# Moving where TensorE's stationary tiles lie in SBUF relative to x

## The chip, the cores and the metric

The kernel runs on one core of one Trainium2 chip. The metric is the device time of one execution in microseconds (us); lower is better. Before the change it is 855.13 us, the median of three runs that lie between 854.54 and 855.58 us.

## What is computed

The inputs q, k and v have 8 batches, 8 heads, 576 positions and 64 features each, in fp32. An attention without a score matrix is followed by a two-layer network:

```python
q_s = softmax(q, axis=features)            # per position
k_s = softmax(k, axis=positions)           # per feature
kv  = einsum('bhsd,bhse->bhde', k_s, v)    # 64x64 per batch and head
x   = einsum('bhsd,bhde->bhse', q_s, kv)   # then laid out as 4608 tokens x 512
h   = x @ w_in                             # 512 -> 2048
g   = h * sigmoid(1.702 * h)
out = g @ w_out                            # 2048 -> 512
```

## The kernel before, in words

**Precision.** Every operand of the two large products is held as a pair, a high part rounded to the type fp32r and a low part that holds what the rounding left, and each product is three fp32r matmuls: high by high, high by low, low by high. On TensorE, a matmul has a stationary operand (128x128, read from SBUF by its own instruction, LDWEIGHTS) and a moving operand (128 rows by 256 or 512 columns, read from SBUF while it streams).

**Tiling.** The 4608 tokens are cut into nine blocks t of 512. The 2048 hidden features are cut into eight pairs p of two groups of 128. In a block, eight steps handle the eight pairs: p goes up from 0 to 7 in even blocks and down from 7 to 0 in odd ones (`pair`, line 384).

**First layer.** In blocks 0 and 1 `plain1` (line 786, matmuls on line 794) takes x whole: 512 moving columns, stationary operand `wj`. In blocks 2 to 8 `ffn1` (line 825, matmuls on line 841) uses seven products of 256 moving columns in place of eight, on sums and differences of the halves of x and of w_in. Product 6, 7, 5 and 4 take their stationary operand from the tile `wt` (sums of w_in), product 1, 2 and 3 from `wj` (w_in itself). Each product is six matmuls, so that a step has 24 with `wt` and 18 with `wj`. The moving operands are the tiles `xo`, which lie in the same places as the tiles `xp` of the first blocks.

**Double buffers.** There are two tiles `wt0` and `wt1`, and two pairs of tiles `wj00`, `wj01` and `wj10`, `wj11`; step p uses those with the number p % 2. They are loaded again from DRAM for each step (`load_kept`, line 389), except where the next step has the same pair.

**Second layer.** `ffn2` (line 889, matmuls on line 904) has the activations `gh` and `gl` as stationary and w_out (`w`, 512 columns) as moving operand: 24 matmuls for each step, interleaved with the first layer's of the next step.

**Attention.** For each block, line 634 forms kv, line 683 transposes q (moving operand: the identity matrix `ident`, stationary operand: `qt`) and line 704 forms x (moving `qT`, stationary `kvn`).

**Order.** The order of the work on each engine comes from `Plan`, a list scheduler with the costs and due times of lines 19 to 125, which runs when the kernel is built. It knows tiles by name and not by address.

**Addresses.** All SBUF tiles come from one pool and are never freed; `sb` (line 193) allocates a tile on its first call, and tiles follow one another in the order of these calls. Nearly all tiles take a multiple of 512 bytes in each partition. The exceptions are the four `vt` and the one `vl` with 2080 bytes, `r`, `qm0` and `qm1` with 32 bytes, and `first` with 64. The first tile, `ident`, begins 128 bytes above a multiple of 512. So the address of every tile modulo 512 is 128 plus the odd bytes of the exceptions that were allocated ahead of it. Addresses inside the tiles of the large products step by multiples of 512, so a tile's residue holds for each matmul that reads it. Before the change, the residues are:

| tile | role | residue modulo 512 | x lies above it by |
|---|---|---|---|
| `xo`, `xp`, `w` | moving, both layers | 448 | - |
| `gh`, `gl` | stationary, second layer | 128 | 320 |
| `wt0` (memory shared with `wide`) | stationary, first layer | 384 | 64 |
| `wj00`, `wj01`, `wj10`, `wj11` | stationary, first layer | 384 | 64 |
| `wt1` (allocated when first used) | stationary, first layer | 448 | 0 |
| `qt`, `qT` | stationary of line 683, moving of line 704 | 256 | - |
| `ident`, `kvn`, `kt` | moving of line 683, stationary of lines 704 and 634 | 128 | - |

Of the kernel before, what the change touches and what calls it, by code (L numbers as in the profile page):

```python
# [10 lines left out]
F32R = mybir.dt.float32r  # L11
# [125 lines left out]
def efficient_attention_then_gelu_ffn(  # L137
# [28 lines left out]
    B, H, S, D = q.shape  # L166
    NTOK, DM = out.shape
    FF = w_out.shape[0]
    P = 128
    C = 4  # L170
# [3 lines left out]
    NP = H // 2  # L174
    KC = DM // P
# [3 lines left out]
    CM = SM // P  # L179
    ST = S - SM  # L180
    W = D + 1
# [11 lines left out]
    def sb(name, shape, dtype=F32, tag=None):  # L193
        return const.tile(shape, dtype, name=name, tag=tag or name)
# [5 lines left out]
    tt = sb("tt", [P, 4, HT])  # L200
    tmp = [sb(f"tmp{i}", [P, DM]) for i in range(2)]
    kt = [sb(f"kt{i}", [P, 2, CM, D]) for i in range(NP)]
    vt = [sb(f"vt{i}", [P, 2, CM, W]) for i in range(NP)]
    qt = [sb(f"qt{i}", [P, C, 2, D]) for i in range(NP)]
    qT = [sb(f"qT{i}", [P, TB]) for i in range(2)]
    mx = [sb(f"mx{i}", [P, 2, D]) for i in range(NP)]
    m1 = sb("m1", [P, 2, 2, D])
    qm = [sb(f"qm{i}", [P, 2 * C]) for i in range(2)]
    r_ = sb("r", [P, 2, NP])
    rs = [r_[:, i] for i in range(2)]  # L210
    kl, vl = sb("kl", [P, H, D]), sb("vl", [P, H, W])
    wj = [[sb(f"wj{i}{jj}", [P, 2, KC, P], F32R) for jj in range(2)] for i in range(2)]
    wts = {}

    def wt(i):
        if i not in wts:
            wts[i] = sb(f"wt{i}", [P, 2, 4, 2 * P], F32R, tag=f"wt{i}")
        return wts[i]


    wide = sb("wide", [P, 4, DM], tag="wt0")
    kept = [[dram.tile([P, 2 * DM], F32, name=f"kept{p}{jj}") for jj in range(2)] for p in range(NS)]
    kept_t = [dram.tile([P, 4 * DM], F32, name=f"kept_t{p}") for p in range(NS)]

# [779 lines left out]
```

## Time and profile before

| what | value |
|---|---|
| median of three runs | 855.13 us |
| the profiled execution's own time | 853.69 us |
| its span (first to last instruction) | 851.9 us |
| TensorE's granted clock | 1.00 of full speed |
| TensorE matmuls busy | 843.5 us |
| VectorE busy | 525.6 us |
| ScalarE busy | 487.2 us |
| GpSimd busy | 114.3 us |

The profile gives for each engine the time in which it was busy, for each group of like instructions their number, their total and their mean duration, and for any stretch of the span the busy time of each engine in it. Matmuls are pipelined: a matmul's own duration is longer than the distance from its start to the next one's start, so the rate of TensorE is read from starts, not from durations. A timeline row gives the start of the first of several like instructions that follow one another, and their number.

### The profile page before, as it was taken

To read this page: it belongs to the slowest core of one execution; us is meant where nothing else is said; L and a number is where in the kernel's file an instruction comes from. 1 tells how busy PE (TensorE), PEld (TensorE's weight loads), DVE (VectorE), ACT (ScalarE), POOL (GpSimd) and SP (SyncE) were. 2 spreads that over 40 slices of the span, in tenths; PEclk is the share of its full clock that TensorE was granted. 3 is DMA by queue.
4 is the path that set the end of the run, shared out by engine and by line. 5 is a ranking of instruction groups with operands and counts; after the bars stand their busy time and mean duration, and the time that the engine had idled before them with its cause. 6 is when DMAs were issued, how large, how long until landed. Compare 5 with 4: busy or idle time off the path is not lost.

```text
span 851.9 us, 14617 instructions
## 1 busy us (share of the span) xinstructions
PE 843.5 (99%) x5643; PEld 722.3 (85%) x5644; DVE 525.6 (62%) x1082; ACT 487.2 (57%) x833; POOL 114.3 (13%) x175
## 2 busy tenths in 40 slices
PE   9999999999999999999999999999999999999998
PEld 4687787778888898888888998899888899889986
DVE  8899896999627875467554765375356533453333
ACT  5799769768537758465744675464356433343322
POOL 1000020120113011111211121100110011101110
PEclk9999999999999999999999999999999999999999
DMA  9999935893479467564845665623654165416541
GB/s 290 283 339 359 265 132 187 263 320 133 129 233 239 129 161 223 173 186 100 246 158 163 165 184 171 177 88 116 204 162 138 50 198 174 148 50 198 173 148 50
DMA packets 127845, 155.63 MB, mean 183 GB/s; under 512 B 76576, under 2 KB 105760, under 8 KB 121376
## 3 DMA queue, kind: packets, MB, share of 16 engines
q0 software_dynamic: 25248, 83.37, 31.7%
q1 hardware_dynamic: 102528, 71.32, 28.2%
q8 instruction: 45, 0.74, 0.4%
q14 instruction: 24, 0.20, 0.1%
HBM read 128.45 MB, written 26.21 MB: 182 GB/s over the span
## 4 chain that ended last, share of the span: by engine, by line
PE 87%; DVE 6%; DMA 4%; ACT 1%; issue 1%; POOL 0%; SPq 0%; DVEq 0%; ACTq 0%; POOLq 0%
PE bank L904 42%; PE bank L841 33%; PE bank L794 5%; DMA raw<-in_moe_w_out 3%; PE bank L634 2%; PE bank L704 2%; PE bank L683 2%; PE bank L296 1%; DVE w L368 1%; DVE gl L812 1%; DVE wide L333 1%; DVE raw L337 0%; PE bank L582 0%; PE bank L583 0%; DMA vt<-in_v 0%
## 5 line engine op out<-in xcount | busy, mean ns | idle before, releaser
L904 PE MATMUL bank<-w,gh 128*128 128x512 f32 x1152 | 361.0, 395 | 0.0
L904 PE MATMUL bank<-w,gl 128*128 128x512 f32 x576 | 226.3, 393 | 0.4 <-DVE gl L812 0.4
L904 PEld LDWEIGHTS bank<-w,gh 128*128 128x128 f32 x1152 | 192.7, 188 | 25.0 <-issue 2.7
L841 PEld LDWEIGHTS bank<-xo,wt 128*128 128x128 f32 x1344 | 187.8, 188 | 17.8
L841 PE MATMUL bank<-xo,wt 128*128 128x256 f32 x1344 | 193.8, 281 | 0.0
L841 PE MATMUL bank<-xo,wj 128*128 128x256 f32 x1008 | 146.2, 280 | 0.5 <-ACT tt L865 0.5
L841 PEld LDWEIGHTS bank<-xo,wj 128*128 128x128 f32 x1008 | 136.3, 188 | 12.1 <-issue 1.6
L854 DVE TENSOR_TENSOR g<-bank,tt 128x256 f32<-128x256 f32 x168 | 71.0, 423 | 102.9 <-PE bank L841 101.3
L904 PEld LDWEIGHTS bank<-w,gl 128*128 128x128 f32 x576 | 108.3, 188 | 24.9 <-DVE gl L812 0.9
L857 ACT ACTIVATE g<-g 128x512 f32<-128x512 f32 x112 | 58.8, 525 | 121.8 <-DVE g L854 118.8
L854 DVE TENSOR_TENSOR tt<-bank,tt 128x256 f32<-128x256 f32 x112 | 47.3, 423 | 130.3 <-PE bank L841 96.3
L397 POOL DMA_DIRECT2D wj<-kept x96 | 59.4, 619 | 364.1 <-PE bank L841 307.0
L794 PE MATMUL bank<-xp,wj 128*128 128x512 f32 x384 | 103.8, 396 | 1.2 <-ACT g L809 0.9
L885 DVE TENSOR_TENSOR gl<-g,gh 128x512 fp32r<-128x512 f32 x112 | 77.3, 691 | 23.3 <-ACT gh L882 22.7
L794 PEld LDWEIGHTS bank<-xp,wj 128*128 128x128 f32 x384 | 71.2, 188 | 19.6 <-ACT g L809 1.3
L882 ACT CAST gh<-g 128x512 fp32r<-128x512 f32 x112 | 69.5, 621 | 3.5
L545 POOL PARTITION_ALL_REDUCE mx<-mx x32 | 32.3, 1009 | 192.9 <-DVE mx L541 167.4
L857 ACT ACTIVATE g<-bank 128x256 f32<-128x256 f32 x56 | 21.6, 386 | 53.3 <-PE bank L841 52.5
L865 ACT COPY tt<-bank 128x256 f32<-128x256 f32 x56 | 20.8, 372 | 50.6 <-PE bank L841 50.3
L397 POOL DMA_DIRECT2D wt<-kept_t x42 | 22.2, 530 | 148.8 <-PE bank L841 148.8
L687 ACT COPY qT<-bank 128x512 f32<-128x512 f32 x36 | 20.5, 588 | 22.3 <-PE bank L683 21.9
L664 ACT ACT_TABLE_LOAD x25 | 32.1, 1283 | 0.4
(103 smaller groups left out, 802.4 us busy)
## 6 DMA issues: line engine op xcount, KB each, us to landing
wt<-kept_t POOLq DMA_DIRECT2D x42, 1024.0 KB, 5.2
wj<-kept POOLq DMA_DIRECT2D x54, 512.0 KB, 3.7
wj<-kept POOLq DMA_DIRECT2D x42, 256.0 KB, 4.9
out<-tmp SPq DMA_DIRECT2D x36, 256.0 KB, 2.8
kt<-in_k SPq DMA_DIRECT2D x32, 256.0 KB, 4.1
raw<-in_moe_w_in SPq DMA_DIRECT2D x16, 512.0 KB, 8.4
raw<-in_moe_w_out SPq DMA_DIRECT2D x16, 512.0 KB, 7.1
kept<-wj SPq DMA_DIRECT2D x16, 512.0 KB, 6.8
```

Of the source, the lines that this page charges most:

```text
L397: "POOL", 1.0, (key,), (ring,), R(t, step - 2, off), lambda: nc.gpsimd.dma_start(out=out(), in_=src), size=size
L545: nc.gpsimd.partition_all_reduce(flat, flat, P, bass_isa.ReduceOp.max)
L664: nc.scalar.activation(x, x, AF.Exp)
L687: plan.add("ACT", act(TB), (PB,), (Q,), rank, lambda: nc.scalar.copy(qT[hp % 2], pq))
L794: nc.tensor.matmul(bank[bk], w[:, l, c, :], x[:, r], start=c == 0 and e == 0, stop=c == KC - 1 and e == 2)
L841: nc.tensor.matmul(ph[bk], w, x[:, r, c, :], start=opens and c == 0 and e == 0, stop=c == 1 and e == 2, skip_group_check=True,)
L854: return lambda: nc.vector.tensor_tensor(out=o, in0=ph[bk], in1=x, op=ALU.add)
L857: return lambda: nc.scalar.activation(o, x, AF.Gelu_apprx_sigmoid)
L865: vec("ACT", act(n), (ZB,), (A,), 2, lambda: nc.scalar.copy(a, ph[Z]))
L882: vec("ACT", act(2 * n), half, H, slot, lambda c=c, gh=gh: nc.scalar.copy(gh, c))
L885: nc.vector.tensor_tensor(out=gl, in0=c, in1=gh.bitcast(F32), op=ALU.subtract)
L904: nc.tensor.matmul(bank[c], l, r, start=first_ and e == 0, stop=last and e == 2)
```

## The change

The four `vt`, `vl`, `r` and the two `qm` (eight exceptions that carry 32 odd bytes each) are no longer allocated in one place ahead of the stationary tiles, but two by two between them, and `wt1` gets its place there too in place of being allocated on first use.

```diff
     kt = [sb(f"kt{i}", [P, 2, CM, D]) for i in range(NP)]
-    vt = [sb(f"vt{i}", [P, 2, CM, W]) for i in range(NP)]
     qt = [sb(f"qt{i}", [P, C, 2, D]) for i in range(NP)]
     qT = [sb(f"qT{i}", [P, TB]) for i in range(2)]
     mx = [sb(f"mx{i}", [P, 2, D]) for i in range(NP)]
     m1 = sb("m1", [P, 2, 2, D])
-    qm = [sb(f"qm{i}", [P, 2 * C]) for i in range(2)]
-    r_ = sb("r", [P, 2, NP])
-    rs = [r_[:, i] for i in range(2)]
-    kl, vl = sb("kl", [P, H, D]), sb("vl", [P, H, W])
-    wj = [[sb(f"wj{i}{jj}", [P, 2, KC, P], F32R) for jj in range(2)] for i in range(2)]
-    wts = {}
+    kl = sb("kl", [P, H, D])
+    wj, wts = [None, None], {}
...
+    def wjs(i):
+        wj[i] = [sb(f"wj{i}{jj}", [P, 2, KC, P], F32R) for jj in range(2)]
+
+    vt = [sb(f"vt{i}", [P, 2, CM, W]) for i in range(2)]
 
     wide = sb("wide", [P, 4, DM], tag="wt0")
+    vt += [sb(f"vt{i}", [P, 2, CM, W]) for i in range(2, NP)]
+    wjs(0)
+    vl = sb("vl", [P, H, W])
+    r_ = sb("r", [P, 2, NP])
+    rs = [r_[:, i] for i in range(2)]
+    wt(1)
+    qm = [sb(f"qm{i}", [P, 2 * C]) for i in range(2)]
+    wjs(1)
```

The residues that follow from it (`xo`, `xp`, `w`, `gh` and `gl` keep theirs):

| tile | residue before | after | x lies above it by, before | after |
|---|---|---|---|---|
| `wt0` | 384 | 192 | 64 | 256 |
| `wj00`, `wj01` | 384 | 256 | 64 | 192 |
| `wt1` | 448 | 320 | 0 | 128 |
| `wj10`, `wj11` | 384 | 384 | 64 | 64 |
| `qt`, `qT` | 256 | 128 | - | - |

The moved `qt` and `qT` bring `ident` from 384 to 0 bytes above its stationary `qt` (line 683), and `qT` from 128 to 0 above its stationary `kvn` (line 704). `vt0` to `vt3` keep their residues. `vl` goes from 352 to 256 and `kl` from 352 to 128. The SBUF in use is the same to the byte. The instructions, their shapes and their order are the same, row by row, on all five engines.

## The prediction

> **What bounds the kernel now.** The page's first part, read before all else, names TensorE; its chain of waits names the two large products as what the end hangs on.
>
> ```profile
> span 851.9 us, 14617 instructions
> PE 843.5 (99%) x5643; PEld 722.3 (85%) x5644; DVE 525.6 (62%) x1082; ACT 487.2 (57%) x833; POOL 114.3 (13%) x175
> ...
> PE 87%; DVE 6%; DMA 4%; ACT 1%; issue 1%; POOL 0%; SPq 0%; DVEq 0%; ACTq 0%; POOLq 0%
> ```
>
> TensorE is busy for 99% of the span and carries 87% of the chain, so the time is a number of matmuls times the distance between their starts. The groups give the numbers.
>
> ```profile
> L904 PE MATMUL bank<-w,gh 128*128 128x512 f32 x1152 | 361.0, 395 | 0.0
> L904 PE MATMUL bank<-w,gl 128*128 128x512 f32 x576 | 226.3, 393 | 0.4 <-DVE gl L812 0.4
> L841 PE MATMUL bank<-xo,wt 128*128 128x256 f32 x1344 | 193.8, 281 | 0.0
> L841 PE MATMUL bank<-xo,wj 128*128 128x256 f32 x1008 | 146.2, 280 | 0.5 <-ACT tt L865 0.5
> ```
>
> Before these four groups TensorE idled 0.9 us in all: it never waits in the stages that the change touches. The 1344 matmuls with wt at 24 for a step make 56 steps, half of them on wt0, half on wt1. What a step costs is read from stretches without attention work. In the last block, whose pairs run from 0 up, the steps begin where the timeline shows the first six matmuls with wt, and the table by stretches, cut there, has wt0 in its rows 1, 3, 5, 7 and wt1 in rows 2, 4, 6 (columns: stretch, length, busy time of PE, PEld, DVE, ACT, POOL with instruction counts, granted clock, DMA share, GB/s).
>
> ```profile
> 758.39:768.92 10.53, 10.53 (x67) 9.46 (x66) 4.69 (x9) 4.10 (x10) 1.79 (x3) 1.00 0.38 118
> 768.92:779.39 10.47, 10.47 (x67) 9.47 (x66) 4.05 (x8) 3.29 (x7) 1.79 (x3) 1.00 0.72 230
> 779.39:789.83 10.44, 10.44 (x67) 9.45 (x66) 3.46 (x7) 3.05 (x7) 1.79 (x3) 1.00 0.57 175
> 789.83:800.25 10.42, 10.42 (x68) 9.41 (x67) 3.49 (x7) 3.05 (x7) 1.79 (x3) 1.00 0.55 183
> 800.25:810.50 10.25, 10.25 (x68) 9.27 (x66) 3.49 (x7) 3.04 (x7) 1.79 (x3) 1.00 0.54 167
> 810.50:821.03 10.53, 10.53 (x67) 9.49 (x66) 3.46 (x7) 3.05 (x7) 1.79 (x3) 1.00 0.57 177
> 821.03:831.56 10.53, 10.53 (x67) 9.46 (x66) 3.45 (x7) 3.06 (x7) 0.00 (x0) 1.00 0.31 110
> ```
>
> Seven steps with the same 66 matmuls, all with TensorE busy throughout at the full granted clock, take from 10.25 to 10.53 us. VectorE's 3.5 us, ScalarE's 3 us and the DMA share of 0.3 to 0.7 leave all three far from binding. So TensorE runs the same work at several rates, and the pattern is regular: a wt0 step takes 10.53, 10.44 or 10.25 us, and the wt1 steps between them lead from one value to the next (10.53 to 10.44 to 10.25 and back to 10.53). I call these three gaits the slow, the middle and the fast phase. A wt0 step hands its phase on: at the turn of blocks 3 and 4 two wt0 steps follow each other, both fast, though VectorE is busy 9.56 and 8.29 us in them. Busy neighbours therefore don't make the difference.
>
> ```profile
> 391.24:401.49 10.25, 10.25 (x67) 9.27 (x66) 9.56 (x22) 6.52 (x13) 2.75 (x3) 1.00 0.12 25
> 401.49:411.75 10.26, 10.26 (x68) 9.27 (x67) 8.29 (x20) 7.42 (x14) 3.80 (x4) 1.00 0.44 115
> ```
>
> The timeline shows it matmul by matmul: the fast and the middle wt0 step, and the wt1 step after the fast one.
>
> ```profile
> 800.25 0.84 PE L841 MATMUL bank<-xo,wt 128*128 128x256 f32 x6
> 800.93 0.84 PE L841 MATMUL bank<-xo,wj 128*128 128x256 f32 x6
> ```
>
> ```profile
> 779.39 0.87 PE L841 MATMUL bank<-xo,wt 128*128 128x256 f32 x6
> 780.10 0.87 PE L841 MATMUL bank<-xo,wj 128*128 128x256 f32 x6
> ```
>
> ```profile
> 810.50 0.88 PE L841 MATMUL bank<-xo,wt 128*128 128x256 f32 x6
> 811.22 0.87 PE L841 MATMUL bank<-xo,wj 128*128 128x256 f32 x6
> ```
>
> Six matmuls take 0.68 us in the fast phase (113 ns each), 0.71 in the middle one (118), and 0.72 on wt1 (120). This is the trace's only evidence that the address matters: wt1 is the only tile to which x lies 0 bytes above, and the only one that changes the phase of undisturbed steps.
>
> **The change part by part.** It removes and adds no instruction, and no engine's order moves. All its cost or gain is in the rate at which TensorE reads.
>
> *Term 1, wt1 from 0 to 128 bytes.* Take 128 to be like 64, the nearest residue that has rows. A wt1 step then costs what a wt0 step costs. Over the three phases a wt0 step costs (10.53 + 10.44 + 10.25) / 3 = 10.407 us, a wt1 step (10.47 + 10.42 + 10.53) / 3 = 10.473. The difference, 0.067 us, times 28 wt1 steps is -1.9 us.
>
> *Term 2, wt0 from 64 to 256 and wj0 from 64 to 192.* No row has these residues. The bounds are the gaits seen: fast throughout, or slow throughout (priced among the rivals). Between them I go by one comparison. At 64 bytes, the 256-column matmuls are dear in two of three phases: middle and slow cost 0.19 and 0.28 us more than fast. The second layer's stationary tiles lie at 320 bytes, and its 512-column matmuls are dear in one phase only: middle and slow differ by 0.09 us with the same 0.71 us per six on line 841. One dear phase fewer saves 0.19 / 3 = 0.063 us per step, for the products whose residue leaves 64 or 0 (42 of a wt0 step's matmuls, 24 of a wt1 step's 42, 79% of all): 0.063 x 56 x 0.79 = 2.8 us. Because that comparison is between different shapes, I count a third: -0.9 us.
>
> *Term 3, the transposes and x.* On line 683 ident comes to lie 0 bytes above qt, on line 704 qT 0 above kvn.
>
> ```profile
> L683 PE MATMUL bank<-ident,qt x144: 270/272/328, 20.0 to 725.0; 128*128 128x128 f32 x144
> L704 PE MATMUL bank<-qT,kvn x256: 216/428/640, 25.7 to 729.2; 64*64 64x512 f32 x16, 64*64 64x64 f32 x16, 64*64 64x448 f32 x16, 64*64 64x128 f32 x16
> ```
>
> The nearest price is wt1's, 0.067 us over 24 matmuls, 2.8 ns each. Times 144 transposes it is 0.4 us; line 704 runs four small matmuls side by side, 64 groups, 0.2 us. Nothing at the least, 0.6 us at the most; I take +0.2, since both are short matmuls with other data types and gaits.
>
> *The other readers of moved tiles.* VectorE reads tiles of several residues at one speed:
>
> ```profile
> L885 DVE TENSOR_TENSOR gl<-g,gh 128x512 fp32r<-128x512 f32 x112 | 77.3, 691 | 23.3 <-ACT gh L882 22.7
> L661 DVE TENSOR_TENSOR qt<-qt,qm 128x512 f32<-128x512 f32 x32 | 22.1, 692 | 1.1
> ```
>
> The first has all operands at 128, the second qt at 256 and qm at 256 or 288: 691 and 692 ns. So VectorE's cost is taken as unchanged; a change of 1% would hide below TensorE, which has 6 us to spare over it in each step. The loads keep their size and go to addresses that are again multiples of 64 bytes; wt's land 5.2 us and wj's 3.7 to 4.9 us after issue, and a step of 10.25 us covers them.
>
> ```profile
> wt<-kept_t POOLq DMA_DIRECT2D x42, 1024.0 KB, 5.2
> wj<-kept POOLq DMA_DIRECT2D x54, 512.0 KB, 3.7
> wj<-kept POOLq DMA_DIRECT2D x42, 256.0 KB, 4.9
> ```
>
> *Sum.* -1.9 - 0.9 + 0.2 = -2.6 us. The profiled execution, 853.69 us with 1.8 us outside its span, would come to 851.1. It lies 1.44 us under the median of the runs shown, so against that median the forecast is 855.13 - 2.6 = 852.5 us.
>
> **The rivals.** *All fast.* Residues from 128 to 256 keep TensorE out of the dear phases altogether. Then a wt0 step gains 10.407 - 10.25 = 0.157 and a wt1 step 10.473 - 10.25 = 0.223 us, times 28 each: -10.6 us, 844.5. For it: the fast gait exists and lasts over whole steps, and the phase that wt1 keeps breaking would no longer be broken. Against it: with 64 bytes, steps stay in the middle or slow gait just as steadily, and wj1 stays at 64. Half of it gives about 850.
>
> *No effect.* The odd gait of wt1 has another source than the residue, or the pattern repeats every 256 bytes, so that wt0 at 256 takes over wt1's place and the 1.9 us with it. Time 855.1, or 855.7 with all of term 3. For it: no product has x 256 bytes above its stationary tile, and the whole address effect is 2% of a matmul. Against it: wt0 and wt1 steps run the same program and only wt1 changes the phase. A rule of the Trainium skill speaks for this rival: "TensorE: Matmul & The Clock Gate", section "Step-by-step: what each phase is for", says that TensorE has two independent read ports to SBUF, so that loading the next weights takes no read bandwidth from the running matmul. By that rule no residue could matter, and the time would stay 855.1; the 0.72 us of wt1 against 0.68 and 0.71 of wt0 disagrees, by little.
>
> *Slower: stuck in the slow phase.* Now every wt1 step moves the phase on, and no phase lasts beyond two steps. With nonzero residues only, a step hands its phase on, so whatever attention's small matmuls leave behind stays until the next of them, and term 3 makes these the only place with a zero residue. If they leave the slow phase, all steps cost 10.53: wt0 steps lose 0.123, wt1 steps 0.057 us, times 28: +5.0 us, 860.1. It decides from the point where the mean step exceeds the (10.407 + 10.473) / 2 = 10.44 of now, which is the middle phase as the rule rather than a third of the time. The same sign comes if 192 and 256 behave like 0 rather than like 64.
>
> **How the numbers follow.** Runs of this kernel differ by 1.04 us, so about 0.2%, 1.7 us, is the least that can be told from no change. My forecast, the zero residue's price gone and the others no worse than 64, gets 0.45, with a range of its own from 850.5 to 854.3; three quarters of it lie beyond 0.2%. All or half fast gets 0.16, no effect 0.16, slower 0.23. That makes faster 0.50, same 0.28, slower 0.22. The range goes from 847.0, which leaves out the full fast lock, to 858.0, which leaves out the full slow one; I give these ends together 2 in 10.
>
> **What would show it.** Right: undisturbed wt1 steps, still recognisable as every second step, take the same 10.25, 10.44 or 10.53 us as the steps around them and no longer change the phase, and more of the steps are fast than a third. Term 1 is wrong if 10.41 to 10.54 still alternate. Term 2 is wrong if wt0 steps with their new residues show values above 10.53, or values other than these three in the direction of slow. Term 3 is wrong if starts on line 683 move apart by over 3 ns. The whole reading is wrong if steps of the same phase differ between blocks without any wait, or if line 794, whose wj0 goes from 64 to 192, differs between wj0 and wj1.

## The result and the profile after

The change makes the kernel slower: 858.59 us (median of six runs, 857.35 to 859.62) against 854.27 us (six runs, 853.07 to 855.58), a ratio of 1.0052 with a 95% interval of 1.0039 to 1.0065, or 4.3 us more. The forecast was 2.6 us less. The profiled execution took 857.35 us.

The page of the changed kernel shows the same program, with TensorE busy for 4.6 us more (843.5 before), its weight loads (PEld) for 2.2 us more, and VectorE, ScalarE and GpSimd within 1.0 us of before. The one matmul more is a record that the trace of before lacks. Lines have moved down by ten, so that 841 is now 851, 904 is 914, 794 is 804 and 683 is 693.

```profile
span 855.5 us, 14618 instructions
PE 848.1 (99%) x5644; PEld 724.5 (85%) x5644; DVE 525.3 (61%) x1082; ACT 488.2 (57%) x833; POOL 114.5 (13%) x175
...
L914 PE MATMUL bank<-w,gh 128*128 128x512 f32 x1152 | 362.6, 396 | 0.0
L914 PE MATMUL bank<-w,gl 128*128 128x512 f32 x576 | 227.3, 395 | 0.0
...
L851 PE MATMUL bank<-xo,wt 128*128 128x256 f32 x1344 | 194.6, 281 | 0.0
...
L851 PE MATMUL bank<-xo,wj 128*128 128x256 f32 x1008 | 146.9, 281 | 0.5 <-ACT tt L875 0.5
...
L804 PE MATMUL bank<-xp,wj 128*128 128x512 f32 x384 | 104.6, 397 | 0.6 <-ACT g L819 0.5
```

There is still no wait to speak of ahead of the large products. Every group shown has become a little dearer, including the two on line 914 whose tiles did not move (361.0 and 226.3 us before). The table by stretches of the last block, cut at the starts of its steps as in the prediction (columns as there; rows 1, 3, 5, 7 use wt0), shows where.

```profile
761.60:772.13 10.53, 10.53 (x67) 9.47 (x66) 4.66 (x9) 4.09 (x10) 1.79 (x3) 1.00 0.42 119
772.13:782.61 10.48, 10.48 (x67) 9.44 (x66) 4.05 (x8) 3.29 (x7) 1.79 (x3) 1.00 0.75 225
782.61:793.17 10.56, 10.56 (x68) 9.49 (x67) 3.45 (x7) 3.07 (x7) 1.79 (x3) 1.00 0.57 173
793.17:803.65 10.48, 10.48 (x68) 9.44 (x66) 3.46 (x7) 3.04 (x7) 1.79 (x3) 1.00 0.56 177
803.65:814.20 10.55, 10.55 (x68) 9.49 (x66) 3.44 (x7) 3.06 (x7) 1.79 (x3) 1.00 0.56 176
814.20:824.68 10.48, 10.48 (x67) 9.44 (x66) 3.46 (x7) 3.04 (x7) 1.79 (x3) 1.00 0.56 172
824.68:835.23 10.55, 10.55 (x67) 9.49 (x66) 3.44 (x7) 3.06 (x7) 0.00 (x0) 1.00 0.32 111
```

The three phases are gone. A wt0 step takes 10.55 us (10.407 before, averaged over the phases), a wt1 step 10.48 (10.473), and no step is fast any more. Over 28 steps of each kind that would make 28 x (0.143 + 0.007) = 4.2 us, an estimate that counts the three phases of before evenly. The same stretch of the program, from the first to the last matmul with `wt`, is read in the list of that line's instructions, first from before and then from after (columns: count, duration min/median/max in ns, first and last start in us):

```profile
L841 PE MATMUL bank<-xo,wt x1344: 274/280/388, 216.9 to 839.1; 128*128 128x256 f32 x192
```

```profile
L851 PE MATMUL bank<-xo,wt x1344: 274/281/385, 217.0 to 842.8; 128*128 128x256 f32 x192
```

It took 622.2 us and takes 625.8. These 3.6 us are all that separates the two profiled executions, whose spans are 851.9 and 855.5 us. The rest of the 4.3 us is that the profiled executions lie under their medians by 0.6 us before and 1.2 us after. The group on line 804 is 0.8 us dearer (103.8 before), but idles 0.6 us less ahead of it (1.2 before), and the first `wt` matmul starts only 0.1 us later.

The mean distance from one matmul's start to the next one's, worked out from the starts of all rows of the trace with waits left out, divides the loss by tile:

| matmuls | residue before, after | distance before | after | difference x count |
|---|---|---|---|---|
| 672 on `wt0` | 64, 256 | 116.40 ns | 118.23 ns | +1.2 us |
| 504 on `wj00`, `wj01` | 64, 192 | 116.42 | 117.61 | +0.6 |
| 672 on `wt1` | 0, 128 | 118.81 | 118.24 | -0.4 |
| 504 on `wj10`, `wj11` | 64, 64 | 116.64 | 117.05 | +0.2 |
| 672 on `gh`, `gl` in wt0 steps | 320, 320 | 230.35 | 232.16 | +1.2 |
| 695 on `gh`, `gl` in wt1 steps | 320, 320 | 230.51 | 231.44 | +0.6 |

So 128 bytes are nearly as bad as 0, 256 and 192 are worse than 64, and the tiles that kept their residues pay too: 2.0 of the table's 3.4 us.

### The profile page after: what moved, and what is told of

It reads as the page before. It is cut to its first block, busy times and chain, and to the rows that moved or that the text cites. A ratio compares the mean times of both kernels' runs of the same rounds, so it can differ in the third digit from the quotient of the medians.

```text
span 855.5 us, 14618 instructions
## 1 busy us (share of the span) xinstructions
PE 848.1 (99%) x5644; PEld 724.5 (85%) x5644; DVE 525.3 (61%) x1082; ACT 488.2 (57%) x833; POOL 114.5 (13%) x175
## 4 chain that ended last, share of the span: by engine, by line
PE 94%; DMA 3%; DVE 2%; issue 0%; ACT 0%; SPq 0%; DVEq 0%
PE bank L914 45%; PE bank L851 33%; PE bank L804 8%; PE bank L644 2%; PE bank L714 2%; DMA raw<-in_moe_w_out 2%; PE bank L693 2%; PE bank L306 1%; DMA raw<-in_moe_w_in 1%; PE bank L592 0%; PE bank L593 0%; DMA out<-tmp 0%; DVE wj L378 0%; DVE kt L566 0%; PE bank L594 0%
## 5 line engine op out<-in xcount | busy, mean ns | idle before, releaser
L867 ACT ACTIVATE g<-g 128x512 f32<-128x512 f32 x112 | 58.8, 525 | 122.7 <-DVE g L864 119.4
```

What stands on the lines that cost most here:

```text
L867: return lambda: nc.scalar.activation(o, x, AF.Gelu_apprx_sigmoid)
```

## The experiments

All runs change only where tiles are allocated; the program, its order and what it computes stay. The edits are against the kernel before, with lines that only move shown by their first words, some of them at their new place alone. In all of them the moving operands stay at 448 modulo 512, and `qt` and `qT` stay at 256. `kl` or `vl` change residue in the `u` and `a` runs with 128, 192, 32 and 96 and in `t1_128`; in the others they don't. Because the moving operands never move, the runs can't tell whether the distance between the two operands counts or the address of the stationary tile by itself. The distances below name the residues either way.

| run | x above `wt0`, `wj0` / `wt1`, `wj1` | w above `gh`, `gl` | undisturbed steps of the last block, us | first to last start on `wt`, us | ratio to before, 95% interval |
|---|---|---|---|---|---|
| before | 64, 64 / 0, 64 | 320 | 10.25 to 10.53 | 622.2 | 1 |
| after | 256, 192 / 128, 64 | 320 | 10.53 to 10.56 and 10.48 | 625.8 | 1.0052 (1.0039 to 1.0065) |
| `u64` | 64 for all | 320 | 10.25 to 10.26 | 616.8 | 0.9929 (0.9904 to 0.9953) |
| `u320` | 320 for all | 320 | 10.25 to 10.26 | 617.1 | 0.9920 (0.9896 to 0.9945) |
| `a64` | 64 for all | 64 | 10.25 to 10.26 | 616.6 | 0.9956 (0.9939 to 0.9973) |
| `u192` | 192 for all | 320 | 10.33 to 10.34 | 620.3 | 1.0000 (0.9980 to 1.0020) |
| `a192` | 192 for all | 192 | 10.40 | 621.3 | 1.0017 (1.0002 to 1.0033) |
| `u128` | 128 for all | 320 | 10.48 and 10.57 to 10.58 | 626.4 | 1.0082 (1.0050 to 1.0114) |
| `a128` | 128 for all | 128 | 10.55 to 10.56 | 628.3 | 1.0110 (1.0090 to 1.0130) |
| `u256` | 256 for all | 320 | 10.54 | 627.1 | 1.0054 (1.0033 to 1.0075) |
| `a256` | 256 for all | 256 | 10.54 to 10.55 | 627.6 | 1.0063 (1.0043 to 1.0082) |
| `u0` | 0 for all | 320 | 10.54 | 627.1 | 1.0061 (1.0043 to 1.0079) |
| `u32` | 32 for all | 320 | 10.48 | 623.7 | 1.0038 (1.0024 to 1.0052) |
| `u96` | 96 for all | 320 | 10.53 to 10.54 | 627.1 | 1.0079 (1.0061 to 1.0098) |
| `mix` | 256, 64 / 64, 64 | 320 | 10.25 to 10.53 | 621.4 | 0.9990 (0.9975 to 1.0005) |
| `t1_128` | 64, 64 / 128, 64 | 320 | 10.26 and 10.47 to 10.48 | 620.5 | 0.9988 (0.9977 to 0.9999) |
| `g256` | 64 for all | 256 | 10.42 to 10.43 | 621.9 | 1.0009 (0.9995 to 1.0024) |

### One residue for the first layer: 64, 128, 192, 256

```diff
# u64
     wide = sb("wide", [P, 4, DM], tag="wt0")
+    wt(1)
```

> One part alone: wt1 gets its place beside wt0, so that x lies 64 bytes above all six stationary tiles of the first layer; qt, qT and everything else stay where they were before. Theory A (a tile's rate hangs on its own residue: 64 and 320 are cheap, since they differ by 256, and 0, 128, 192 and 256 are dear) and theory B (what is dear is to switch between tiles of different residues) expect the same here: the steps with wt1 cost what those with wt0 cost, 10.25, 10.44 or 10.53 us, none changes the phase, and the time falls by 1.9 us from 854.3 to about 852.4.

```diff
# u128: qm allocated last
-    qm = ...
     r_ = ...
     kl, vl, wj, wide = ...
+    wt(1)
+    qm = ...
```

> x lies 128 bytes above all six stationary tiles; qt and qT as before. Theory A: the rate that wt1 has at 128 in the changed kernel, 118.2 ns for each 256-column matmul, holds for all of them, undisturbed steps cost about 10.5 us, about 858 us. Theory B: one residue for all is as good as 64 for all, steps of 10.25, 10.44 and 10.53 us that keep their phase, about 852.4 us.

```diff
# u192: kl ahead, then the stationary tiles, then qm, r and vl
-    qm, r_, vl = ...
     kl, wj, wide = ...
+    wt(1)
+    qm, r_, vl = ...
```

> x lies 192 bytes above all six stationary tiles; qt and qT as before. Theory A: the rate that wj0 has at 192 in the changed kernel, 117.6 ns, for all, and 231.7 ns for the 512-column matmuls on line 794 against 229.1 before, about 857.5 us. Theory B: as with 64 for all, about 852.4 us.

```diff
# u256: the stationary tiles after two of the four vt
+    vt = [... for i in range(2)]
+    wj, wide = ...
+    wt(1)
+    vt += [... for i in range(2, NP)]
     qt, qT, mx, m1, qm, r_, kl, vl = ...
```

> x lies 256 bytes above all six stationary tiles; qt and qT as before. Theory A: the rate that wt0 has at 256 in the changed kernel, 118.2 ns, for all, steps of 10.5 us, about 858.5 us. Theory B: as with 64 for all, about 852.4 us.

Moving `wt1` alone from 0 to 64 gains three times what the forecast gave it: 848.08 us against 854.37, where 852.4 was expected by both theories. The table by stretches of the last block of `u64`, first four steps:

```profile
754.40:764.65 10.25, 10.25 (x67) 9.27 (x66) 4.76 (x9) 4.12 (x9) 1.79 (x3) 1.00 0.42 122
764.65:774.90 10.25, 10.25 (x67) 9.27 (x66) 4.09 (x8) 3.32 (x8) 1.79 (x3) 1.00 0.75 232
774.90:785.16 10.26, 10.26 (x68) 9.27 (x66) 3.49 (x7) 3.06 (x7) 1.79 (x3) 1.00 0.57 178
785.16:795.41 10.25, 10.25 (x67) 9.27 (x66) 3.49 (x7) 3.05 (x7) 1.79 (x3) 1.00 0.57 180
```

With no tile at 0, the fast phase, once reached, is kept: of the 25 undisturbed steps in blocks 2 to 8, the first two steps left out (10.46 and 10.53 us), 22 take 10.25 us and three, each right after a step with attention work, 10.44 or 10.52. That is the mechanism of the prediction's rival "All fast", with wt1 at 64 rather than at 128.

Theory B, that one residue for all is cheap whatever it is, falls with `u128` and `u256`: 861.37 and 858.74 us (theory A expected 858 and 858.5), steps of 10.48 to 10.58 us. Theory A put 192 among the dear ones; `u192` took 853.93 us, as long as before and what neither theory expected (857.5 and 852.4), and its steps in the last block, 10.33 us, lie nearer to the fast ones (in other blocks, 10.59 occurs too). So 192 stands between.

### 320, 0, both layers at 192, and one dear tile

```diff
# u320: the stationary tiles first
+    wj, wide = ...
+    wt(1)
     vt, qt, qT, mx, m1, qm, r_, kl, vl = ...
```

> x lies 320 bytes above all six stationary tiles of the first layer, as it does above the second layer's gh and gl. Theory C, from the four runs so far (multiples of 128 are dear in themselves; 64, 192 and 320 are not; and passing between tiles whose residues differ modulo 256 costs a few ns each time): as with 64 for all, undisturbed steps mostly of 10.25 us, about 848 us. Theory D (only a short distance such as 64 is good, since 192 gained nothing in the median): steps of 10.33 us and more, 854 us or above.

```diff
# u0: first, 64 bytes, ahead of the stationary tiles
     kl, vl = ...
+    first = sb("first", [P, 16])
     wj, wide = ...
+    wt(1)
-    first = sb("first", [P, 16])
```

> x lies 0 bytes above all six stationary tiles of the first layer. Theory C: dear as wt1 before, 118.8 ns for every 256-column matmul in place of 116.4 to 116.6 on the other tiles, and no fast steps: +1.6 for wt0, +1.2 and +1.1 for wj0 and wj1, about 858.5 us. Theory B (one residue for all is cheap whatever it is), already hurt by 128 and 256: about 848 us.

```diff
# a192: as u192, with gh and gl just ahead of wj
-    gs = ...
     kl = ...
+    gs = ...
     wj, wide = ...
+    wt(1)
```

> x lies 192 bytes above the first layer's stationary tiles, as in the run with 192 for all six, and w also lies 192 bytes above the second layer's gh and gl (320 in all runs so far). Theory C: no passage between residues is left, so the two dear matmuls at the head of each run of six (122 and 116 ns in the run with 192) and the 233 ns of the last 512-column matmul ahead of them go, undisturbed steps fall from 10.33 to 10.25 us, about 848 us. Rival E (192 has a price of its own): nothing changes, 10.33 us, about 854 us.

```diff
# mix: wt0 after two of the four vt, all others as in u64
+    vt = [... for i in range(2)]
+    wide = ...
+    vt += [... for i in range(2, NP)]
     qt, qT, mx, m1, qm, r_, kl, vl, wj = ...
+    wt(1)
```

> As in the run with 64 for all six, but wt0 alone at 256. Theory F (a dear tile costs only its own matmuls): wt0's 672 matmuls go from 115.3 to 118.9 ns, +2.4 us on 848.1, about 850.5 us; steps with wt1 stay at 10.25 us. Theory G (a dear tile also breaks the fast phase for the tiles that stayed): wt1, wj0, wj1 and the 512-column matmuls on line 904 get slower too, steps with wt1 alternate between the three gaits again, 853 to 855 us.

`u320` (848.11 us) equals `u64` (848.08) in every step of the last block, and `u0` (859.65) equals `u256` (858.74) step by step. The second step of the last block, from `u256` and from `u0`:

```profile
772.85:783.39 10.54, 10.54 (x67) 9.51 (x66) 4.05 (x8) 3.31 (x7) 1.79 (x3) 1.00 0.70 225
```

```profile
774.18:784.72 10.54, 10.54 (x68) 9.51 (x67) 4.05 (x8) 3.31 (x7) 1.79 (x3) 1.00 0.75 223
```

What counts is therefore the residue modulo 256, not 512, as far as these two pairs show it: 64 and 320 are one case, 0 and 256 another.

`a192` refutes the part of theory C on passages. With no passage between residues left, its steps take 10.40 us, not 10.25. The last block's first step of `u192`, and then of `a192`:

```profile
763.83:774.16 10.33, 10.33 (x67) 9.34 (x66) 4.75 (x9) 4.12 (x9) 1.79 (x3) 1.00 0.40 117
```

```profile
760.01:770.41 10.40, 10.40 (x67) 9.36 (x66) 4.73 (x9) 4.10 (x9) 1.79 (x3) 1.00 0.40 121
```

192 has a price of its own, as rival E says, and putting `gh` and `gl` there too raised it above the 10.33 us that E expected. Matmuls of both lengths pay. In the step of `a192` shown, the starts of the 24 with 512 columns are 232.0 ns apart and those of the 24 with `wt` 115.9, against 228.9 and 113.3 in the same step of `u64`; each kind adds about 0.07 us. On line 794 (795 in that run), they are 233.2 ns apart with `wj0` at 192, against 229.1 at 64.

`mix` decides between theories F and G. It is the kernel before with the roles of the two `wt` exchanged, one dear tile among five at 64, and its steps show the values of before with the roles exchanged: now the wt0 steps (rows 1, 3, 5, 7) move the phase, the wt1 steps hand it on.

```profile
758.18:768.60 10.42, 10.42 (x68) 9.41 (x67) 4.74 (x9) 4.09 (x9) 1.79 (x3) 1.00 0.41 117
768.60:778.85 10.25, 10.25 (x68) 9.27 (x66) 4.09 (x8) 3.32 (x8) 1.79 (x3) 1.00 0.76 230
778.85:789.38 10.53, 10.53 (x67) 9.49 (x66) 3.45 (x7) 3.06 (x7) 1.79 (x3) 1.00 0.57 181
789.38:799.91 10.53, 10.53 (x67) 9.46 (x66) 3.45 (x7) 3.06 (x7) 1.79 (x3) 1.00 0.56 177
799.91:810.38 10.47, 10.47 (x67) 9.47 (x66) 3.46 (x7) 3.03 (x7) 1.79 (x3) 1.00 0.55 170
810.38:820.82 10.44, 10.44 (x67) 9.45 (x66) 3.47 (x7) 3.05 (x7) 1.79 (x3) 1.00 0.57 177
820.82:831.24 10.42, 10.42 (x68) 9.41 (x67) 3.49 (x7) 3.06 (x7) 0.00 (x0) 1.00 0.32 112
```

The median is 853.38 us, 5.3 us above `u64`, of which wt0's own matmuls, 3.5 ns dearer (118.8 against 115.3), explain 2.4. Most of the rest is paid by tiles that did not move: wt1, wj0 and wj1 go from about 115.2 to 116.2 ns, 1.7 us over 1680 matmuls, and the second layer's matmuls rise by about 0.5 ns. Theory G holds.

### Term 1 alone, the second layer at 256, and finer steps

```diff
# t1_128: wt0 stays at 384, wt1 at 320, both pairs of wj at 384
-    qm = ...
     r_, kl, vl = ...
+    wt(1)
+    qm = ...
     wj, wide = ...
```

> Term 1 of the prediction by itself: wt1 goes from 0 to 128 bytes, all other tiles stay where they were before (64; qt and qT too). The prediction: 128 is like 64, -1.9 us, about 852.3. Theory H (the residue counts modulo 256, and 0, 128 are both dear; one dear tile also keeps the others out of the fast gait): wt1's matmuls stay at 118 ns, the others at 116 to 117, steps between 10.4 and 10.55 us, 853.5 to 855, no change that can be told.

```diff
# g256: as u64, with gh and gl after two of the four vt
-    gs = ...
+    vt = [... for i in range(2)]
+    gs = ...
+    vt += [... for i in range(2, NP)]
```

> As with 64 for all six of the first layer, but gh and gl, the second layer's stationary tiles, 256 bytes below w in place of 320. Theory H: mixing residues that differ modulo 256 breaks the fast gait for the 256-column matmuls, which stayed at 64: 116 to 118 ns in place of 115.1, so 852 to 856 us. Rival I (512-column matmuls are cheaper at 256: line 794 took 227.7 ns there against 229.1 at 64, so 1728 matmuls gain 1.4 ns, 2.4 us): 845.7 us.

```diff
# u96: vl after the stationary tiles
     qm, r_, kl = ...
-    vl = ...
     wj, wide = ...
+    wt(1)
+    vl = ...
```

> x lies 96 bytes above all six stationary tiles of the first layer, half way between the cheap 64 and the dear 128. If the price follows lines of 64 bytes, 96 is as cheap as 64, about 848 us; if it follows lines of 32 bytes, it has a price of its own between 848 and 861 us. Theory H says only that it differs from gh's residue modulo 256 by 32, so passages cost a little: 849 to 855 us.

```diff
# u32: as u96, and first ahead of the stationary tiles
+    first = sb("first", [P, 16])
     wj, wide = ...
+    wt(1)
+    vl = ...
-    first = sb("first", [P, 16])
```

> x lies 32 bytes above all six stationary tiles of the first layer, half way between the dear 0 and the cheap 64. If the price follows lines of 64 bytes, 32 is as dear as 0, about 859.5 us, or as cheap as 64, 848; if it follows lines of 32 bytes, it lies between. Theory H: 849 to 858 us.

`t1_128` is the prediction's first term by itself. It gives 852.66 us, a ratio of 0.9988, about 1.0 us less than before and not 1.9. The steps show why (last block, first four; rows 1 and 3 use wt0):

```profile
758.93:769.19 10.26, 10.26 (x67) 9.27 (x66) 4.77 (x10) 4.13 (x9) 1.79 (x3) 1.00 0.39 120
769.19:779.67 10.48, 10.48 (x68) 9.43 (x66) 4.05 (x8) 3.33 (x8) 1.79 (x3) 1.00 0.71 224
779.67:789.93 10.26, 10.26 (x68) 9.28 (x67) 3.49 (x7) 3.04 (x7) 1.79 (x3) 1.00 0.59 177
789.93:800.40 10.47, 10.47 (x67) 9.43 (x66) 3.45 (x7) 3.05 (x7) 1.79 (x3) 1.00 0.58 180
```

wt1 at 128 is as dear as at 0 (118.2 ns against 118.8). But it breaks the phase in another way than 0 does: after a wt1 step at 128, the next wt0 step mostly comes out fast (of the 14 undisturbed wt0 steps after the first, 11 take 10.25 or 10.26 us). So the gain is made by wt0 steps, and wt1 steps stay at 10.47. In the changed kernel, this is of no use, because wt0 itself is at 256.

This run also prices the rest of the change. The changed kernel differs from `t1_128` only in `wt0`, `wj0`, `qt`, `qT`, `kl` and `vl`. Its stretch is 5.3 us longer (625.8 against 620.5), and its ratio to before is higher by 0.0064, which is 5.5 us. So the 4.3 us are about 1.0 us gained by moving wt1 and some 5.3 us lost by moving the others.

`g256` refutes rival I: 854.35 us. The steps of the first layer at 64 go from 10.25 to 10.43 us when `gh` and `gl` alone are at a dear residue. With 860.08 us for 96 and 857.02 us for 32, no line of 64 bytes is to be seen, and for 96 the 849 to 855 us of theory H fail as well: of the residues tried, 64 (and 320) alone is cheap, and 32 bytes on either side are dear.

### What was still open: both layers at one residue

```diff
# a128, a256, a64: as u128, u256, u64, with gh and gl just ahead of wj
-    gs = ...
+    gs = ...
     wj, wide = ...
```

> x and w lie 128 bytes above all stationary tiles of both layers. Theory J (128 is dear in itself, wherever the others lie): steps of 10.45 us and more, 856 to 862 us, as with 128 for the first layer alone. Theory K (what made 128 dear is that gh and gl stayed at 320, a different residue modulo 256): steps fall to 10.25 us, about 848 us.

> x and w lie 256 bytes above all stationary tiles of both layers. Theory J: 256-column matmuls stay at 119 ns, those of 512 columns at 228 to 231, steps of 10.45 us and more, 855 to 860 us. Theory K: 10.25 us, about 848 us.

> x and w lie 64 bytes above all stationary tiles of both layers; gh and gl thus go from 320 to 64. With a period of 256 bytes (theories J and K alike) nothing changes against 64 for the first layer alone: steps of 10.25 us, about 848 us. If the period is 512 bytes for the 512-column matmuls, line 904 leaves its 229 ns and the time differs by over 1 us for each ns.

The second step of the last block of `a128` and of `a256`:

```profile
778.77:789.33 10.56, 10.56 (x68) 9.46 (x67) 4.05 (x8) 3.31 (x7) 1.79 (x3) 1.00 0.74 232
```

```profile
773.50:784.05 10.55, 10.55 (x68) 9.51 (x67) 4.05 (x8) 3.31 (x7) 1.79 (x3) 1.00 0.76 225
```

Theory J holds. 128 and 256 are dear even where nothing lies at another residue, 863.23 and 858.62 us. `u128` and `a128` lose more than the table's stretch shows (7.0 and 9.4 us by their ratios, 4.2 and 6.1 us in the stretch). Their 512-column matmuls in the first two blocks, some 744, are 1.5 to 3.3 ns dearer than before, which makes about 2 us. In the two profiled executions, the first start on `wt` comes at 223.1 and 221.4 us in place of 216.9, and 30 us of that part show a granted clock of 0.89, against 1.00 before; how much of the medians this explains stays open. `a64` has the steps of `u64`, so 320 and 64 are the same for the second layer too. Its median, 850.42 us, lies 2.3 us above that of `u64`, but the stretch from the first to the last start on `wt` is the same (616.6 and 616.8 us); what differs between executions outside it stays open.

## Why the prediction was wrong, point by point

**What bounds the kernel** was right: TensorE's rate is all that moved, and no wait came or went in the changed stages.

**The three phases** were read rightly for the kernel before. A step without a dear tile hands its phase on, and `wt1` at 0 was what broke it (`u64`). The sum then bounded the new residues by the values of these phases, and the wt0 steps of the changed kernel, 10.55 us, lie outside them.

**Term 1 failed at "Take 128 to be like 64, the nearest residue that has rows".** wt1 at 128 costs 118.2 ns, not 116.4 (`t1_128`). By itself, the term was worth 1.0 us and not 1.9, and that was earned by the wt0 steps. The working was also too small where it was right: removing a dear tile was priced as wt1 steps that become like the wt0 steps of before, but `u64` gains 6.1 us (0.0071 of 854.37), because the wt0 steps become fast too. The rival "All fast" named this and priced it at 10.6 us.

**Term 2 had the wrong sign.** Its step was to read the second layer's 320 bytes as a long distance and to conclude that longer is cheaper. 320 is 64 once more (`u320`, `a64`). Taking wt0 and wj0 off 64 cost about 5.3 us in the changed kernel (after against `t1_128`), where the term expected 0.9 us gained; from all tiles at 64, taking wt0 off costs 5.3 us alone (`mix` against `u64`).

**What term 2 left out.** It counts only the products whose residue changes (79%) and has nothing for those whose tiles stay. The second layer's matmuls, on `gh` and `gl`, pay 1.8 us, as much as wt0 and wj0 themselves (1.2 + 0.6).

**Term 3** was of the right sign and smaller than the value taken: starts on line 683 went from 108.7 to 108.9 ns, 0.03 us over 144, and the distances on line 704 grew by 0.1 us in all.

**The other readers** were right: VectorE's row that had qt at 256 is unchanged with qt at 128.

```profile
L671 DVE TENSOR_TENSOR qt<-qt,qm 128x512 f32<-128x512 f32 x32 | 22.1, 692 | 1.1
```

**The rivals.** The slower one had the size (5.0 us against 4.3) but not the main mechanism. The kernel did not get stuck in the slow phase by what attention leaves behind; it has no common phase left, as wt0 steps at 10.55 us and wt1 steps at 10.48 alternate. What happened is nearer to that rival's last sentence, that 192 and 256 behave like 0 rather than like 64 (256 does; 192 lies between), which deserved to be a rival of its own with the price of the zero residue on more tiles: 2.4 ns for the 1176 matmuls of wt0 and wj0 is 2.8 us, with nothing gained on wt1. "No effect" had half of it, a pattern that repeats every 256 bytes. The Trainium skill ("TensorE: Matmul & The Clock Gate", "Step-by-step: what each phase is for") says that loading the next weights takes no read bandwidth from the running matmul, which spoke for that rival. The runs show that the stationary tile's address matters all the same: 859.65 us in `u0` against 848.08 in `u64`, with stretches of 627.1 and 616.8 us. Whether the load and the running matmul disturb each other, or one of the two is slower by itself, is not shown. The loads' own durations on line 841 hardly differ, with means of 187.7 ns in `u64` and 188.6 (`wt`) and 189.2 (`wj`) in `u0`.

**The range** reached to 858.0 us and the result is 858.59. A mean step of 10.53 us was priced, as the rival stuck in the slow phase, at 860.1 us, and the range left it out. The mean step of the changed kernel in the last block, (10.55 + 10.48) / 2 = 10.515 us, comes close to that value, by another way.

**The signs.** Two of the named signs came: wt0 steps above 10.53 us (term 2 wrong), and a difference on line 794 (now 804), where the starts are 231.6 ns apart with `wj0` and 230.6 with `wj1`. The second says less than the prediction took it to say, because they also differ in `u256` (227.5 and 228.7), where all six tiles have one residue.

## What to carry to other kernels

Where TensorE is busy throughout and loads a stationary tile for every matmul, look at the distance of starts, matmul by matmul, and sort it by the addresses of the two operands; two gaits for the same instruction can be a sign that placement matters. Put all stationary tiles of such a stretch at one good residue, and find it by trial: one tile at a bad residue also slows its neighbours (`mix`), and one bad residue for all (`u128`, `a128`, `u96`) was slower than the spread of the changed kernel. Here the one-line version, `wt(1)` right after `wide`, puts all tiles of the first layer at 64 bytes and takes 848.08 us, 0.9929 of before (0.9904 to 0.9953); `u320` with 848.11 us is its equal.

## What the runs showed of the hardware

With fp32r operands, 128 stationary columns and 256 moving ones, the distance between starts depends on the residue of the stationary tile modulo 256 bytes. With the moving operand at one place in all runs, and named by how far it lies above the stationary one, the starts are 113.3 ns apart in the fast phase at 64 (115.1 to 115.3 on average over a run with 64 for all), and on average 115.6 to 116.3 at 192, 117.9 to 118.0 at 32, 118.1 to 118.9 at 128, 118.7 to 118.8 at 96 and 118.4 to 119.4 at 0 and 256. For 512 moving columns the order is another: starts on the line of the first blocks are 227.2 to 227.8 ns apart with 256 for all tiles of both layers (`a256`), 229.0 to 229.1 with 64 (`a64`), 232.2 to 232.5 with 128 (`a128`) and 232.9 to 233.2 with 192 (`a192`). At 64 the same matmuls run in three rhythms, steps of 10.25, 10.44 and 10.53 us; undisturbed steps were seen to hand on the first and the last, and a step with attention's small matmuls can change the rhythm. Why these residues and not others could not be told from these traces: apart from lines of 64 bytes, which 96 and 32 spoke against, no model was tested.
